# Attention scores: one fp32 product of q and k in place of three f32r products of split values

## The chip, the cores and the metric

The kernel runs on one core of one Trainium2 chip. The metric is the device time of one execution in microseconds; the median of three runs is given.

## The reference

Three layers follow one another: attention with normalised q and k, a gated feed-forward layer, and a soft mixture of experts. Only the first lines matter here:

```python
q_n, k_n = (rmsnorm(q, g_q), rmsnorm(k, g_k))          # q, k: 4 x 12 x 448 x 64
scores = scale * np.matmul(q_n, k_n.transpose(0, 1, 3, 2))
scores = scores - np.max(scores, axis=-1, keepdims=True)
attn = np.exp(scores)
attn = attn / (np.sum(attn, axis=-1, keepdims=True) + 1e-09)
return np.matmul(attn, v).astype(np.float32)
# then x (1792 x 768) -> silu(x @ w_gate) * (x @ w_val) @ w_out  (d_ff 1536) -> soft MoE, 8 experts, 4 slots each
```

## The kernel before

**Attention.** The 4 batches x 12 heads are worked on in 24 pairs of heads (`pairs`, index i). A pair has four steps c = 0..3, one for each block of query rows (three of 128 rows, a last of 64), so there are 96 attention steps t = 4i + c. The two heads of a pair lie in partitions 0 to 63 and 64 to 127 (`halves`). For a block with c < 3 the scores of the two heads are two matmuls that use the two halves of TensorE's rows (L493), each with 64 rows of contraction, 128 weight columns and 448 moving columns. For c = 3 the last 64 query rows of both heads stand in one zero-padded tile `qz`, and one matmul with 128 rows serves both heads (L497).

**The split.** f32r is a matmul type that keeps fewer bits of a 32-bit float. To keep precision, q and k are each stored as a high part, as f32r rounds it, and a low part (the value minus the high part). `qa` and `ka` hold two planes, high and low, and `scores` adds up three products a block: high x high, high x low, low x high. Per pair, after TensorE has transposed q and k into PSUM (`tq`, L424), `transp_hi` writes the high planes with ScalarE (L454 for q with the gain, L456 for k), and `transp_lo` writes the low planes with VectorE (L465 for q, and L65 inside `sub_lo` for k) and then copies the last 64 columns of both planes of q into `qz` (L474; in the first twelve pairs one half by VectorE and one by GpSimd, later both by GpSimd). The PSUM tile `tq` is one of three that rotate (`pt_tile`); the transposes of the probabilities (`tp`, L572) use the same three, so they wait until both parts have read `tq`.

**After the scores.** VectorE takes the negated row maximum (`smax`, L508), ScalarE the exponential (`sexp`, L520). In the first 12 pairs TensorE transposes the probabilities (L572) and the product with v runs at L595; in the later 12 pairs VectorE transposes and the product runs at L630.

**Order of the work.** It is written out by hand: each step is a list of short names (`ORDA`, `ORD0`, `ORDB` for the steps t < 28, `ORD1` and the following lists afterwards), in which S is `scores`, TH is `transp_hi`, TL or L is `transp_lo`, TP or T the transposes of q and k. Each engine works through its instructions in this order. In steps t < 28 the kernel also rebuilds the feed-forward weights from their 64-bit form on ScalarE, GpSimd (`hneg` L213, `hpos` L219) and VectorE (`raw` L228), and stores them. From t = 28 on (`M0`) each step also runs one block of the feed-forward layer: 18 f32r matmuls with 128 x 128 weights and 448 columns (`gv`, L696). After the 96 attention steps the feed-forward steps go on alone, and last come the experts, whose weights stream in from memory.

Of the kernel before, what the change touches and what calls it, by code (L numbers as in the profile page):

```python
# [8 lines left out]
F32 = mybir.dt.float32  # L9
F32R = mybir.dt.float32r  # L10
# [4 lines left out]
AF = mybir.ActivationFunctionType  # L15
ALU = mybir.AluOpType
# [5 lines left out]
def attn_moe_softmoe_kernel(  # L22
# [15 lines left out]
    nc = tc.nc  # L38
    B, H, S, HD = q.shape
# [5 lines left out]
    P = 128  # L45
    CP = 112
    NC = S // CP
    NP = H // 2
# [9 lines left out]
    EV = dict(v=nc.vector.tensor_copy, a=nc.scalar.copy, p=nc.gpsimd.tensor_copy)  # L58
# [5 lines left out]
    def sub_lo(dst, src, hi):  # L64
        nc.vector.tensor_tensor(out=dst, in0=src, in1=hi.bitcast(F32), op=ALU.subtract)  # L65
# [13 lines left out]
    def s_tile(n):  # L79
        return ps.tile([P, S], F32, tag=f"s{n}", name="s")  # L80
# [10 lines left out]
    ap_ = tc.alloc_tile_pool(name="attn", bufs=1, side="right")  # L91
# [6 lines left out]
    gsc = cpool.tile([P, 1], F32, name="gsc")  # L98
# [203 lines left out]
    NPR = len(pairs)  # L302
    NT_ = NPR * NC
    st = {}
# [11 lines left out]
    NX = 2 * NP  # L316
# [113 lines left out]
    halves = [slice(0, HD), slice(HD, P)]  # L430


    QL = S % P
    qz = [ap_.tile([P, 2, 2 * QL], F32R, name=f"qz{n}") for n in range(2)]

    def qz_zeros():
        for n in range(2):
            nc.vector.memset(qz[n].bitcast(F32), 0.0)

    def qk_tiles(i):  # L440
        d = st[i]
        if "qa" not in d:
            d["qa"] = ap_.tile([P, 2, S], F32R, tag="qa", name="qa", bufs=2)
            d["ka"] = ap_.tile([P, 2, S], F32R, tag="ka", name="ka", bufs=2)
        return d["qa"], d["ka"]

    def transp_hi(i, n):

        if i >= NPR:
            return  # L450
        tq = st[i]["qk"[n]]
        qa, ka = qk_tiles(i)
        if n == 0:
            nc.scalar.activation(out=qa[:, 0], in_=tq[:, :S], func=AF.Copy, scale=gsc[:, 0:1])  # L454
        else:
            (EV[ENG["hid"]] if i < NP else nc.scalar.copy)(out=ka[:, 0], in_=tq[:, :S])  # L456

    def transp_lo(i, n):

        if i >= NPR:  # L460
            return
        tq = st[i].pop("qk"[n])
        qa, ka = qk_tiles(i)
        if n == 0:
            nc.vector.scalar_tensor_tensor(  # L465
                out=qa[:, 1],
                in0=tq[:, :S],
                scalar=gsc[:, 0:1],
                in1=qa[:, 0].bitcast(F32),
                op0=ALU.mult,  # L470
                op1=ALU.subtract,
            )
            for j, r in enumerate(halves):
                EV[ENG["qz"][j] if i < NX else "p"](out=qz[i % 2][r, :, QL * j : QL * j + QL], in_=qa[r, :, S - QL :])  # L474
        else:
            sub_lo(ka[:, 1], tq[:, :S], ka[:, 0])

    def scores(t):

        i, c = divmod(t, NC)  # L480
        d = st[i]
        qa, ka = qk_tiles(i)
        if t < M0 and t % 2:
            sc = [ps.tile([P, S], F32, tag=g, name="s") for g in "gv"[: both(t)]]
        elif t < M0 or i >= NX:
            sc = [s_tile(j) for j in range(2)]
        else:
            sc = [s_tile((2 * (t - M0) + j) % 3) for j in range(2)]
        terms = ((0, 0), (0, 1), (1, 0))
        for n, (wt, mv) in enumerate(terms):  # L490
            if c < NC - 1:
                for j, r in enumerate(halves):
                    nc.tensor.matmul(  # L493
                        sc[j], qa[r, wt, c * P : (c + 1) * P], ka[r, mv, :], start=(n == 0), stop=(n == 2)
                    )
            else:
                nc.tensor.matmul(sc[0], qz[i % 2][:, wt], ka[:, mv], start=(n == 0), stop=(n == 2))  # L497
        d[c] = {"sc": sc, "sm": ap_.tile([P, 2], F32, tag="sm", name="sm", bufs=4), "pr": {}}

    def both(t):  # L500

        return 1 if t % NC == NC - 1 else 2
# [631 lines left out]
    def step0(t):  # L1134
# [8 lines left out]
        def S_():  # L1143
            if t + 1 < M0:
                scores(t + 1)
# [30 lines left out]
        def TH():  # L1176
            if 0 <= ct_ < 2:
                transp_hi(i + 1, ct_)

        def TL():  # L1180
            if 0 <= ct_ < 2:
                transp_lo(i + 1, ct_)
# [101 lines left out]
    def step(t):  # L1284
# [48 lines left out]
        def S_():  # L1333
            if att:
                scores(t)
# [5 lines left out]
        def TH():  # L1341
            if ev is not None:
                transp_hi(i + 1, ev)

        def L_():
            if ev is not None:
                transp_lo(i + 1, ev)
# [208 lines left out]
    ENG = dict(rel0="ap", rel1="aa", top0="p", top1="pp", wl1="pv", wh1="a", hid="a", pvd="avavavaa", pvd1="vavavava", nm="pp", qz="vp", rb="a", xh="a", wpa="aa", wpq="a")  # L1556
# [32 lines left out]
    with tc.manual_schedule():  # L1589
        load(0, "qk")  # L1590
        load(1, "qk")
        setup()
        setup_stack()
        qz_zeros()
        fill(16)
        loads = dict(
# [14 lines left out]
        for n in range(2):  # L1611
            norm_mul(0, n, nc.vector)
            transp(0, n)
            transp_hi(0, n)
            fill(PF[n])
            if n == 0:
                norm_ss(1, (1,))
        load(2, "qk")
        w_load(2)
        for n in range(2):  # L1620
            norm_rs(1, (n,))
            norm_mul(1, n, nc.gpsimd)
            transp_lo(0, n)
        w_relu(0, (0,))
        scores(0)
        fill(4)
        for t in range(NT_ + 4):
            step(t)
            if t == 4:
                for n in range(4):  # L1630
                    nc.sync.dma_start(
                        out=ph32[32 * n : 32 * n + 32], in_=phi.rearrange("(d a) s -> a d s", a=32)
# [30 lines left out]
    with tc.manual_schedule():  # L1663
# [18 lines left out]
        for c in range(KD):  # L1682
# [4 lines left out]
                start=True,  # L1687
                stop=True,
# [68 lines left out]
        for u, (e, i, n) in enumerate(eunits):  # L1757
            w = wtile.pop(u)
            if i == 0:
                if n == 0:  # L1760
                    hacc[e] = s_tile(e % 3)[:, :FQ]
                for c in range(KD2 * n, KD2 * n + KD2):
                    for j in range(4):
                        if e < E - 2:

                            mv = w(c % KD2, 2 * FQ * (j // 2), 2 * FQ)
                            mv = mv.rearrange("p (q a t) -> p a q t", a=2, t=2)[:, j % 2]
                        else:
                            mv = w(c % KD2, FQ * j, FQ)
# [3 lines left out]
                if n == 1:  # L1773
# [10 lines left out]
                    for t in range(2):  # L1784
                        nc.vector.tensor_copy(
                            out=h1m.rearrange("p (j t) s -> p t j s", t=2)[:, t, :, SPE * e : SPE * e + SPE],
                            in_=ht_[:, P * t : P * t + P].rearrange("p (j s) -> p j s", j=4)[
                                :, :, SPE * e : SPE * e + SPE
                            ],
                        )  # L1790
                    h1s[e] = h1m
            else:
                if i == 1:
                    for kh_ in range(KH2 * n, KH2 * n + KH2):
                        for j in range(4):
# [4 lines left out]
                                start=(e == 0 and kh_ == 0),  # L1800
                                stop=(e == E - 3 and kh_ == KH - 1),
# [56 lines left out]
```

## Time and profile before

| | us |
|---|---|
| median of 3 runs | 763.62 (762.92 to 764.35) |
| profiled execution, its own time | 762.68 |
| span of the profiled execution, first to last instruction | 760.8 |
| TensorE busy in the span | 726.9 (96%) |
| VectorE busy | 463.4 (61%) |
| ScalarE busy | 392.2 (52%) |
| GpSimd busy | 439.4 (58%) |
| mean granted TensorE clock | 0.993 of full speed |

Busy time of TensorE counts each matmul from its start to the modelled end of its result, so consecutive matmuls overlap in the record. The time that a matmul costs in a dense stream is therefore read from start to start, not from its duration.

### The profile page before, as it was taken

To read this page: it belongs to the slowest core of one execution; us is meant where nothing else is said; L and a number is where in the kernel's file an instruction comes from. 1 tells how busy PE (TensorE), PEld (TensorE's weight loads), DVE (VectorE), ACT (ScalarE), POOL (GpSimd) and SP (SyncE) were. 2 spreads that over 40 slices of the span, in tenths; PEclk is the share of its full clock that TensorE was granted. 3 is DMA by queue.
4 is the path that set the end of the run, shared out by engine and by line. 5 is a ranking of instruction groups with operands and counts; after the bars stand their busy time and mean duration, and the time that the engine had idled before them with its cause. 6 is when DMAs were issued, how large, how long until landed. Compare 5 with 4: busy or idle time off the path is not lost.

```text
span 760.8 us, 20681 instructions
## 1 busy us (share of the span) xinstructions
PE 726.9 (96%) x8580; PEld 566.5 (74%) x8580; DVE 463.4 (61%) x914; ACT 392.2 (52%) x839; POOL 439.4 (58%) x382
## 2 busy tenths in 40 slices
PE   7899999999999999999999999999999999888884
PEld 6566667787778777888888788888879888655552
DVE  5989988788877866677677777666234123420013
ACT  5888888887788644455444454544232222300112
POOL 8978867766676965778686775844444443000100
PEclk9999999999999999999999999999999999999998
DMA  7677576746675642544335432444247997899998
GB/s 234 193 238 227 181 226 212 224 158 202 212 252 172 195 124 70 156 146 126 92 113 157 145 83 74 124 133 133 85 142 254 384 384 245 314 425 421 413 368 262
DMA packets 74237, 157.84 MB, mean 207 GB/s; under 512 B 9376, under 2 KB 49312, under 8 KB 71328
## 3 DMA queue, kind: packets, MB, share of 16 engines
q1 hardware_dynamic: 73424, 155.49, 61.2%
q8 instruction: 67, 1.10, 0.6%
q10 hardware_dynamic: 720, 1.03, 0.4%
q14 instruction: 26, 0.21, 0.1%
HBM read 136.84 MB, written 19.66 MB: 206 GB/s over the span
## 4 chain that ended last, share of the span: by engine, by line
PE 77%; DMA 9%; POOL 5%; DVE 4%; issue 3%; ACT 1%; ACTq 0%; SPq 0%; POOLq 0%; DVEq 0%
PE pg L696 44%; DMA w<-in_moe_w_dram 7%; PE s L493 6%; PE xp L630 6%; PE tp L572 3%; PE tq L424 2%; PE s L595 2%; PE sp L887 2%; POOL hpos L219 2%; PE xp L595 2%; PE s L497 1%; POOL ri L392 1%; PE lp L770 1%; PE wpp L268 1%; PE s L1770 1%
## 5 line engine op out<-in xcount | busy, mean ns | idle before, releaser
L696 PE MATMUL pg<-xh,wh 128*128 128x448 f32 x576 | 219.3, 381 | 0.0
L696 PE MATMUL pg<-xl,wh 128*128 128x448 f32 x576 | 210.8, 366 | 0.0
L520 ACT ACTIVATE pr<-s,sm 128x448 f32<-128x448 f32 x168 | 106.2, 635 | 113.3 <-DVE sm L508 109.5
L696 PE MATMUL pg<-xh,wl 128*128 128x448 f32 x432 | 158.5, 367 | 0.3 <-POOL wl L255 0.3
L696 PEld LDWEIGHTS pg<-xh,wh 128*128 128x128 f32 x576 | 108.2, 188 | 21.9 <-issue 10.0
L255 POOL TENSOR_TENSOR wl<-raw,wh 128x768 fp32r<-128x768 f32 x60 | 111.1, 1861 | 11.1 <-ACT wh L247 10.9
L696 PEld LDWEIGHTS pg<-xl,wh 128*128 128x128 f32 x576 | 108.5, 188 | 8.6 <-issue 0.6
L247 ACT CAST wh<-raw 128x768 fp32r<-128x768 f32 x96 | 79.0, 836 | 58.9 <-PE pg L696 34.9
L537 POOL TENSOR_SCALAR pr<-pr,su 128x448 f32<-128x448 f32 x84 | 54.8, 663 | 81.5 <-DVE su L533 35.1
L508 DVE TENSOR_REDUCE sm<-s 128x1 f32<-128x448 f32 x168 | 98.0, 613 | 2.3 <-PE s L493 1.0
L219 POOL TENSOR_TENSOR hpos<-hpos,hneg 128x768 f32<-128x768 f32 x36 | 66.1, 1835 | 40.1 <-ACT hneg L210 35.7
L696 PEld LDWEIGHTS pg<-xh,wl 128*128 128x128 f32 x432 | 81.1, 188 | 7.5 <-POOL wl L255 0.7
L255 POOL TENSOR_TENSOR raw<-raw,wh 128x768 fp32r<-128x768 f32 x23 | 42.4, 1843 | 54.0 <-ACT wh L247 54.0
L392 POOL TENSOR_TENSOR ri<-ss,mhalf 128x16 f32<-128x16 f32 (+2 forms) x26 | 70.5, 2712 | 2.2
L493 PE MATMUL s<-ka,qa 64*128 64x448 f32 x432 | 63.3, 397 | 0.4 <-DVE ka L65 0.2
L725 DVE SCALAR_TENSOR_TENSOR ht<-ht,pg 128x448 f32<-128x448 f32 x40 | 24.7, 619 | 60.2 <-ACT ht L718 60.2
L616 DVE STREAM_TRANSPOSE pT<-pr 128x448 f32<-128x448 f32 x84 | 52.8, 628 | 5.1 <-POOL pr L537 4.8
L572 PE MATMUL tp<-ident,pr 128*112 128x128 f32 x336 | 49.8, 278 | 5.6 <-DVE qa L465 2.0
L696 PE MATMUL pg<-xh,raw 128*128 128x448 f32 x144 | 52.7, 366 | 0.0
L572 PEld LDWEIGHTS tp<-ident,pr 128*112 128x112 f32 x336 | 36.1, 133 | 21.9 <-issue 7.2
L493 PEld LDWEIGHTS s<-ka,qa 64*128 64x128 f32 x432 | 34.9, 184 | 21.1 <-issue 11.7
L398 POOL TENSOR_TENSOR qn<-qk,ri 128x512 f32<-128x512 f32 (+1 forms) x46 | 50.1, 1090 | 0.9
(216 smaller groups left out, 1162.4 us busy)
## 6 DMA issues: line engine op xcount, KB each, us to landing
w<-in_moe_w_dram SPq DMA_DIRECT2D x22, 1536.0 KB, 12.6
raw<-w SPq DMA_DIRECT2D x72, 384.0 KB, 5.4
w<-raw SPq DMA_DIRECT2D x36, 384.0 KB, 3.2
vt<-in_v_dram SPq DMA_DIRECT2D x60, 224.0 KB, 4.0
r<-in_moe_w_out_dram SPq DMA_DIRECT2D x12, 768.0 KB, 5.0
r<-in_moe_w_gate_dram SPq DMA_DIRECT2D x12, 768.0 KB, 6.2
r<-in_moe_w_val_dram SPq DMA_DIRECT2D x12, 768.0 KB, 5.1
w<-in_moe_w_dram SPq DMA_DIRECT2D x24, 384.0 KB, 9.8
```

The costliest lines, as they stand in the source:

```text
L219: eng.tensor_tensor(out=hp, in0=hp, in1=hn, op=ALU.subtract)
L247: (EV[ENG["wh1"]] if u - NO < NU else nc.scalar.copy)(out=wh, in_=wst[u]["raw"])
L255: eng.tensor_tensor(out=wl, in0=wst[u]["raw"], in1=wst[u]["wh"].bitcast(F32), op=ALU.subtract)
L392: nc.gpsimd.tensor_tensor(out=ri, in0=ss, in1=mhalf[:p, : len(ns)], op=ALU.pow)
L398: eng.tensor_tensor(out=st[i]["qn"][:, n].rearrange("p c h d -> p h c d"), in0=st[i]["qk"][: rows(i), n], in1=st[i]["ri"][:, n] .rearrange ...
L493: nc.tensor.matmul(sc[j], qa[r, wt, c * P : (c + 1) * P], ka[r, mv, :], start=(n == 0), stop=(n == 2))
L508: nc.vector.tensor_reduce(out=d["sm"][:, j : j + 1], in_=d["sc"][j], axis=AX.X, op=ALU.max, negate=True)
L520: nc.scalar.activation(out=p, in_=d["sc"][j], func=AF.Exp, bias=d["sm"][:, j : j + 1], accum_out=st[i]["su"][:, c, j : j + 1])
L537: nc.gpsimd.tensor_scalar(out=p, in0=p, scalar1=su[:, j : j + 1], scalar2=1.0, op0=ALU.mult, op1=ALU.mult)
L572: nc.tensor.transpose(tp[:CP, ck * P : (ck + 1) * P], pr[:, ck * CP : (ck + 1) * CP], ident)
L616: nc.vector.transpose(out=pT[:, 6 - c if j else c, :], in_=st[i][c]["pr"].pop(j))
L696: nc.tensor.matmul(d[r], wt[:, P * c : P * c + P], mv, start=(c == 0 and n == 0), stop=(c == KD - 1 and n == 2),)
```

## The change

q and k are written once each, by ScalarE, as plain fp32 (`transp_hi` keeps its two instructions, with fp32 as the output type). The two VectorE instructions that make low parts go. `transp_lo` only copies the last 64 columns of q into `qz`, one plane in place of two, and reads `qa` instead of following the low part; it does nothing for k. `scores` issues one fp32 matmul a head (c < 3) or a block (c = 3), where three f32r matmuls were added up in PSUM. The order lists are as they were. The tiles `qa`, `ka` and `qz` have half their size.

```diff
-    qz = [ap_.tile([P, 2, 2 * QL], F32R, name=f"qz{n}") for n in range(2)]
+    qz = [ap_.tile([P, 2 * QL], F32, name=f"qz{n}") for n in range(2)]
...
-            d["qa"] = ap_.tile([P, 2, S], F32R, tag="qa", name="qa", bufs=2)
-            d["ka"] = ap_.tile([P, 2, S], F32R, tag="ka", name="ka", bufs=2)
+            d["qa"] = ap_.tile([P, S], F32, tag="qa", name="qa", bufs=2)
+            d["ka"] = ap_.tile([P, S], F32, tag="ka", name="ka", bufs=2)
...
     def transp_hi(i, n):
...
         if n == 0:
-            nc.scalar.activation(out=qa[:, 0], in_=tq[:, :S], func=AF.Copy, scale=gsc[:, 0:1])
+            nc.scalar.activation(out=qa, in_=tq[:, :S], func=AF.Copy, scale=gsc[:, 0:1])
         else:
-            (EV[ENG["hid"]] if i < NP else nc.scalar.copy)(out=ka[:, 0], in_=tq[:, :S])
+            (EV[ENG["hid"]] if i < NP else nc.scalar.copy)(out=ka, in_=tq[:, :S])
 
     def transp_lo(i, n):
...
-            nc.vector.scalar_tensor_tensor(
-                out=qa[:, 1],
-                in0=tq[:, :S],
-                scalar=gsc[:, 0:1],
-                in1=qa[:, 0].bitcast(F32),
-                op0=ALU.mult,
-                op1=ALU.subtract,
-            )
-            for j, r in enumerate(halves):
-                EV[ENG["qz"][j] if i < NX else "p"](out=qz[i % 2][r, :, QL * j : QL * j + QL], in_=qa[r, :, S - QL :])
-        else:
-            sub_lo(ka[:, 1], tq[:, :S], ka[:, 0])
+        if i >= NPR or n:
+            return
+        qa, ka = qk_tiles(i)
+        for j, r in enumerate(halves):
+            EV[ENG["qz"][j] if i < NX else "p"](out=qz[i % 2][r, QL * j : QL * j + QL], in_=qa[r, S - QL :])
...
-        terms = ((0, 0), (0, 1), (1, 0))
-        for n, (wt, mv) in enumerate(terms):
-            if c < NC - 1:
-                for j, r in enumerate(halves):
-                    nc.tensor.matmul(
-                        sc[j], qa[r, wt, c * P : (c + 1) * P], ka[r, mv, :], start=(n == 0), stop=(n == 2)
-                    )
-            else:
-                nc.tensor.matmul(sc[0], qz[i % 2][:, wt], ka[:, mv], start=(n == 0), stop=(n == 2))
+        if c < NC - 1:
+            for j, r in enumerate(halves):
+                nc.tensor.matmul(sc[j], qa[r, c * P : (c + 1) * P], ka[r, :], start=True, stop=True)
+        else:
+            nc.tensor.matmul(sc[0], qz[i % 2], ka, start=True, stop=True)
```

## Rows read from the trace of the kernel before

**Rows 1.** The page's part 1: busy us (share of span), instructions of two engines.
```profile
PE 726.9 (96%) x8580; PEld 566.5 (74%) x8580; DVE 463.4 (61%) x914; ACT 392.2 (52%) x839; POOL 439.4 (58%) x382
```

**Rows 2.** Stretches: length; PE, PEld, DVE, ACT, POOL busy us (count); clock; DMA share; GB/s.
```profile
11.00:32.00 21.00, 16.25 (x141) 11.20 (x139) 17.90 (x28) 17.95 (x40) 19.72 (x18) 1.00 0.62 198
32.00:43.00 11.00, 9.81 (x76) 6.23 (x76) 9.63 (x18) 9.16 (x21) 8.78 (x9) 1.00 1.00 278
43.00:113.00 70.00, 68.96 (x1023) 45.77 (x1021) 64.56 (x110) 60.38 (x145) 55.09 (x42) 1.00 0.69 214
113.00:530.00 417.00, 416.64 (x4791) 336.44 (x4790) 304.74 (x608) 248.55 (x531) 290.95 (x253) 1.00 0.49 151
...
655.00:760.80 105.80, 83.32 (x1522) 52.30 (x1514) 18.59 (x57) 16.64 (x41) 4.76 (x12) 0.95 0.97 370
```

**Rows 3.** Groups by line, TensorE: output<-inputs, rows*columns, output xcount | busy us, mean ns | idle.
```profile
L493 PE MATMUL s<-ka,qa 64*128 64x448 f32 x432 | 63.3, 397 | 0.4 <-DVE ka L65 0.2 <-ACT ka L456 0.2
...
L497 PE MATMUL s<-ka,qz 128*128 128x448 f32 x72 | 19.7, 382 | 0.0
```

**Rows 4.** Timeline of TensorE around one block of scores (c < 3): start us, us, what.
```profile
259.61 0.37 PE L696 MATMUL pg<-xh,wl 128*128 128x448 f32 x1
259.90 0.88 PE L493 MATMUL s<-ka,qa 64*128 64x448 f32 x6
260.71 0.47 PE L696 MATMUL pg<-xh,wh 128*128 128x448 f32 x1
261.02 0.37 PE L696 MATMUL pg<-xl,wh 128*128 128x448 f32 x1
```

**Rows 5.** Timeline of TensorE around one block of scores with c = 3.
```profile
264.51 0.76 PE L497 MATMUL s<-ka,qz 128*128 128x448 f32 x3
265.11 0.36 PE L696 MATMUL pg<-xh,wh 128*128 128x448 f32 x1
```

**Rows 6.** Timeline of TensorE around the two first fp32 matmuls of L794.
```profile
278.89 1.02 PE L794 MATMUL lt<-lg,stack 128*128 128x448 f32 x2
...
279.95 0.37 PE L696 MATMUL pg<-xl,wh 128*128 128x448 f32 x1
...
559.21 0.36 PE L696 MATMUL pg<-xh,raw 128*128 128x448 f32 x1
559.41 0.91 PE L794 MATMUL lt<-lg,stack 128*128 128x448 f32 x2
...
560.36 0.36 PE L696 MATMUL pg<-xl,wh 128*128 128x448 f32 x1
```

**Rows 7.** Timeline of TensorE: fp32 matmuls of L1740 in four tiles of 32 rows.
```profile
747.79 0.42 PE L1740 MATMUL op<-ext,w 32*112 32x192 f32 x2 [0.32 <-DVE w L1747]
747.80 0.41 PE L1740 MATMUL s<-ext,w 32*112 32x192 f32 x1
747.81 0.56 PE L1740 MATMUL op<-ext,w 32*112 32x192 f32 x3
748.06 0.32 PE L1740 MATMUL s<-ext,w 32*112 32x192 f32 x1
```

**Rows 8.** Timeline of TensorE, 10 to 116 us: entries with idle time before them [us <-releaser].
```profile
32.08 1.08 PE L572 MATMUL tp<-ident,pr 128*112 128x128 f32 x8 [1.23 <-ACT pr L520]
42.54 0.62 PE L572 MATMUL tp<-ident,pr 128*112 128x128 f32 x4 [1.11 <-DVE qa L465]
65.06 0.62 PE L572 MATMUL tp<-ident,pr 128*112 128x128 f32 x4 [0.36 <-DVE hT L583]
```

**Rows 9.** Groups by line, VectorE, 10 to 110 us: the two that make low parts.
```profile
L465 DVE SCALAR_TENSOR_TENSOR qa<-tq,gsc,qa 128x448 fp32r<-128x448 f32 x8 | 5.4, 680 | 1.7 <-ACT qa L454 1.7
L65 DVE TENSOR_TENSOR ka<-tq,ka 128x448 fp32r<-128x448 f32 x8 | 4.9, 610 | 0.5 <-ACT ka L456 0.5
```

**Rows 10.** Timeline of VectorE at 41 us: an instruction and the wait before it.
```profile
40.84 0.96 DVE L228 SCALAR_TENSOR_TENSOR raw<-r,hpos 128x768 uint32<-128x768 uint32 x1 [1.21 <-POOL hpos L219]
```

**Rows 11.** Groups by line, GpSimd, 10 to 110 us: the copies into `qz`.
```profile
L474 POOL CAST qz<-qa 64x128 fp32r<-64x128 f32 x8 | 2.3, 288 | 10.0 <-DVE qa L465 9.8
```

More of the change, by code (lines that the diff above doesn't have):

```diff
@@ L433, in attn_moe_softmoe_kernel @@
     QL = S % P
-    qz = [ap_.tile([P, 2, 2 * QL], F32R, name=f"qz{n}") for n in range(2)]
+    qz = [ap_.tile([P, 2 * QL], F32, name=f"qz{n}") for n in range(2)]
     def qz_zeros():
         for n in range(2):
-            nc.vector.memset(qz[n].bitcast(F32), 0.0)
+            nc.vector.memset(qz[n], 0.0)
     def qk_tiles(i):
@@ L442, in qk_tiles @@
         if "qa" not in d:
-            d["qa"] = ap_.tile([P, 2, S], F32R, tag="qa", name="qa", bufs=2)
-            d["ka"] = ap_.tile([P, 2, S], F32R, tag="ka", name="ka", bufs=2)
+            d["qa"] = ap_.tile([P, S], F32, tag="qa", name="qa", bufs=2)
+            d["ka"] = ap_.tile([P, S], F32, tag="ka", name="ka", bufs=2)
         return d["qa"], d["ka"]
     def transp_hi(i, n):
[L449 to L453, printed above, removed]
-            nc.scalar.activation(out=qa[:, 0], in_=tq[:, :S], func=AF.Copy, scale=gsc[:, 0:1])
-        else:
-            (EV[ENG["hid"]] if i < NP else nc.scalar.copy)(out=ka[:, 0], in_=tq[:, :S])
-    def transp_lo(i, n):
         if i >= NPR:
@@ L464, in transp_lo @@
         if n == 0:
-            nc.vector.scalar_tensor_tensor(
-                out=qa[:, 1],
-                in0=tq[:, :S],
-                scalar=gsc[:, 0:1],
-                in1=qa[:, 0].bitcast(F32),
-                op0=ALU.mult,
-                op1=ALU.subtract,
-            )
-            for j, r in enumerate(halves):
-                EV[ENG["qz"][j] if i < NX else "p"](out=qz[i % 2][r, :, QL * j : QL * j + QL], in_=qa[r, :, S - QL :])
-        else:
-            sub_lo(ka[:, 1], tq[:, :S], ka[:, 0])
+            nc.scalar.activation(out=qa, in_=tq[:, :S], func=AF.Copy, scale=gsc[:, 0:1])
+        else:
+            (EV[ENG["hid"]] if i < NP else nc.scalar.copy)(out=ka, in_=tq[:, :S])
+    def transp_lo(i, n):
+        if i >= NPR or n:
[3 more added lines that the diff above has]
+            EV[ENG["qz"][j] if i < NX else "p"](out=qz[i % 2][r, QL * j : QL * j + QL], in_=qa[r, S - QL :])
     def scores(t):
```

## The prediction

> **What bounds the kernel now.** I read the page's busy times first: TensorE 96%, VectorE 61% [rows 1]. Such a mean hides stages, so the second view is the busy time by stretch [rows 2]. From 113 to 530 us, where attention and the feed-forward layer run together, TensorE is busy 416.64 of 417.00 us; from 43 to 113 us, the later steps of the head, 68.96 of 70.00. Only before 43 us has it gaps: 4.75 us between 11 and 32 us, 1.19 us between 32 and 43 us. There GpSimd (19.72 of 21.00 us) and VectorE (17.90) are the full ones. After 655 us the kernel waits for expert weights (DMA share 0.97). So work taken from VectorE pays only before 43 us, and time added to TensorE is paid almost everywhere the scores run. Busy is not proof of a dense stream, as ends are modelled, so the third view is the timeline, read from start to start; in it the f32r matmuls of L696 follow each other at about 0.205 us (261.02 to the row after a block, less the load that is named below) [rows 4].
>
> **The price of a block of scores, before.** For c < 3 six matmuls run as three passes, two heads side by side in TensorE's row halves: from the block's first start, 259.90, to the next matmul's, 260.71, is 0.81 us [rows 4]. It splits into 3 passes of about 0.205 (0.615 us) and 0.19 us at the two ends. For c = 3 three matmuls follow the stream with no gap: 264.51 to 265.11, 0.60 us [rows 5]. There are 432 / 6 = 72 blocks of the first kind and 72 / 3 = 24 of the second [rows 3], four a pair of heads.
>
> **The price after.** An fp32 matmul with 448 columns is not in the scores yet, but L794 is one: 128 x 128 weights, 448 columns, two records. In the middle of a stream the f32r matmul before it starts at 559.21, it starts at 559.41, and the second f32r matmul after it starts at 560.36 [rows 6]. From 559.41 to 560.36 is 0.95 us, of which one f32r pass takes 0.205: the fp32 matmul costs 0.745 to 0.75 us, 0.375 a record. That is the c = 3 block as it will be: 0.75 - 0.605 = +0.145 us.
>
> For c < 3 the question is whether the two heads still run side by side and whether the 0.1 us at each end stays. Side by side: the four row tiles of L1740 are fp32, and records of four different tiles start between 747.79 and 747.81 us, the next at 748.06 [rows 7]; so row tiles overlap in fp32. The ends: the other L794 matmul comes straight after a row-tiled block, and takes 278.89 to 279.95 with one f32r pass, 1.06 us, 0.105 more than in the stream [rows 6]; that is the load of the first weights that nothing covers once the tiling changes, and fp32 does not hide it. So both ends stay, and the block goes from 0.615 to 0.75 us of passes: +0.14 us. The number of weight loads falls from three to two a tile, but they lie under the passes in both kernels (next paragraph).
>
> The Trainium skill (TensorE: Matmul & The Clock Gate, section Part 3: Packing small matmuls, The mechanism) says that a weight load overlaps matmuls in flight only when it goes to another row group. By that rule every pass would pay its load, and two long passes with two loads would cost what three short passes with three loads cost. The trace does not agree: the f32r matmuls of one tile start 0.205 us apart with a load each, and L794's two records take 0.75 us together [rows 4, 6].
>
> **How many blocks pay.** From 32.08 us on TensorE has hardly a gap, so a block behind that point moves everything behind it. Steps 7 to 95 lie there: 66 blocks with c < 3 and 23 with c = 3. 66 x 0.143 + 23 x 0.145 = 12.8 us (0.143 is the middle of 0.135, from 0.75 less 0.615, and 0.15, from 0.75 less 0.60). The six blocks of steps 1 to 6 fall where TensorE waits for others and cost nothing; if that cover were gone they would cost 6 x 0.143 = 0.9 us.
>
> **What comes back.** VectorE loses 24 x 2 instructions, 0.68 and 0.61 us each [rows 9], 31 us in all, and the copies into `qz` are halved. In the stretch from 113 to 530 us VectorE is busy 304.74 of 417.00 us and TensorE waits for nobody [rows 2], so 17 of the 24 pairs give nothing back. In the head I take the waits one by one [rows 8]:
> - 42.54 us, 1.11 us, the transposes of probabilities wait until the low part of q has read the PSUM tile. The low part goes, the tile is free once ScalarE has read it, and TensorE itself is the next late one: -1.1 us.
> - 65.06 us, 0.36 us, and one more wait of the same kind 28 us later: they wait for a VectorE copy in a run of VectorE work that holds low parts: 2 x 0.36, -0.7 us.
> - 32.08 us, 1.23 us, and the smaller waits before it (4.75 us of gaps between 11 and 32 us [rows 2]): they end on ScalarE or GpSimd, and GpSimd is busy 19.72 of 21.00 us. VectorE's own rebuild of weights waits for GpSimd too, 1.21 us at 40.84 us [rows 10]. GpSimd loses at most half of each copy into `qz`, 0.14 of 0.288 us [rows 11], and three of them lie before 40 us: at most 0.4 us. Its waits for the low part of q in front of these copies, 9.8 us in all [rows 11], end sooner, but GpSimd's gaps in the stretch to 32 us are only 1.3 us [rows 2]. If all gaps to 32 us went instead, 4.75 us less the 0.9 us of passes would come back, 3.8 us; if nothing, 0. I take -0.3, near zero, since GpSimd keeps its work.
>
> ScalarE keeps its two instructions a pair at the same shapes; a plain fp32 output instead of a rounded one I cost at nothing between -0.05 and +0.05 us each, and ScalarE (248.55 of 417.00 us, [rows 2]) hides it. `scores` no longer waits for VectorE but for ScalarE, which is earlier in every step; no wait is added and no queue is passed. The stage after 530 us has no score work; its weight stream starts when attention's memory comes free, so it moves along with TensorE.
>
> Sum: 12.8 - 1.1 - 0.7 - 0.3 = +10.7 us. The profiled execution took 762.68 us (span 760.8 and 1.9 around it), so 773.4 after; the median of the runs lies 0.94 us above the profiled one, so I predict 763.62 + 10.7 = 774.3 us. The forecast's own range: all gaps of TensorE from 11 us on recovered (4.75 + 1.19 + 1.04 = 7.0 us against 95 blocks, 13.6 us) gives +6.6, 770.2; nothing recovered and nothing covered gives +13.7, 777.3.
>
> **The rivals.**
> - *The load at the block's border is hidden under a longer fp32 pass* in 64-row tiles. Then 0.105 us of each c < 3 block comes back: 12.8 - 66 x 0.105 - 2.1 = +3.8 us, 767.4. For: a record of 0.375 us is longer than a load. Against: L794 after a row-tiled block still pays 0.105 us [rows 6].
> - *The head is bound by VectorE* and shrinks by what VectorE loses, so the kernel is not slower. From 10 to 110 us the low parts are 5.4 + 4.9 us [rows 9], and half of eight copies into `qz` is an estimated 8 x 0.14 = 1.1 us at GpSimd's price [rows 11], 11.4 us; only the 68 blocks of steps 28 to 95 would pay, 9.8 us: -1.6 us, 762.0. For: VectorE is busy 64.56 of 70.00 us from 43 to 113 us [rows 2]. Against: TensorE is busy 68.96 us of the same 70.00, and shows 7.0 us of gaps in the whole head. It decides from the point where the head gives back more than 1.4 us a pair (9.8 / 7).
> - *Loads are not covered in fp32 row tiles or in f32r ones*, the rule named above as a mechanism of this kernel: three passes of 0.187 and three loads of 0.187 us (0.375 / 2 as the clean pass) make 1.12 us, two records and two loads the same, so the passes cost nothing and only the 2.1 us come back: 761.5. The rows speak against it.
> - *The two heads no longer overlap in fp32.* Then each c < 3 block takes 0.75 us more: 10.7 + 66 x 0.75 = +60 us, 834. L1740 speaks against it [rows 7].
> - *The product is not carried out as two fp32 records* but in a single pass: 89 x 0.41 us less than before, about 727. L794 and L1740 speak against it [rows 6, 7].
>
> **How the numbers follow.** The forecast gets 0.83, the border rival 0.07, VectorE's head 0.03 (at the edge: half of it faster by over 0.2%, half within), the load rule 0.02 (faster), the loss of overlap 0.03, the single pass 0.01, and 0.01 is left. A change of 0.2%, 1.5 us, is about what a measurement of this kernel can tell from none. So faster 0.05, same 0.02, slower 0.93. The range reaches from 767.0, which takes in the border rival, to 778.0, just past the forecast's upper end.
>
> **What would show it.** In the profile after, the scores should have 288 records of 64 rows and 48 of 128 rows in place of 432 and 72; a c < 3 block among L696 should take 0.95 us from its first start to the next matmul in place of 0.81, a c = 3 block 0.75 in place of 0.60. The stretch of steps 28 to 95 should be 9.8 us longer, VectorE's busy time some 31 us shorter, and step 10's scores should start close to where they did, 43.5 us. TensorE should still have no gap after that. If the stretch from step 28 to 95 grows by less than 6 us, the price of the passes is wrong; if it grows as said and the total does not, the head gave back more than its gaps.

## The result and the profile after

The changed kernel takes 771.12 us in the median of six runs, the kernel before 763.27 us in the runs beside it: a ratio of 1.0097, with an interval from 1.0071 to 1.0123. A second series of both gave 1.0123 (1.0102 to 1.0144). So the change costs 7 to 9 us, about 1%. The profiled execution after took 773.55 us, the longest of its six, with a span of 771.8 us.

The page's part 1 after the change shows TensorE 11.3 us busier and VectorE 26.3 us less busy than [rows 1]:

```profile
PE 738.2 (96%) x8412; PEld 547.7 (71%) x8412; DVE 437.1 (57%) x866; ACT 391.3 (51%) x839; POOL 441.4 (57%) x382
```

Busy times by stretch after, in the columns of [rows 2]; 114.8 us is now the start of step 28 and 540 us that of step 95, where they were 113 and 530:

```profile
11.00:32.00 21.00, 16.82 (x128) 10.02 (x126) 16.78 (x23) 17.32 (x37) 19.73 (x18) 1.00 0.64 190
32.00:43.00 11.00, 10.17 (x73) 6.00 (x74) 9.31 (x17) 8.86 (x23) 10.44 (x9) 1.00 1.01 300
43.00:114.80 71.80, 70.95 (x990) 42.22 (x987) 58.84 (x102) 60.45 (x145) 57.90 (x42) 1.00 0.68 207
114.80:540.00 425.20, 425.01 (x4668) 323.24 (x4668) 286.33 (x574) 248.14 (x531) 288.36 (x253) 1.00 0.49 148
666.00:771.80 105.80, 82.82 (x1544) 51.95 (x1515) 18.96 (x58) 17.02 (x42) 4.77 (x12) 0.97 0.98 373
```

Before 32 us GpSimd is as full as it was, 19.73 us against 19.72. From 43 us on TensorE has no more room than before; the stretch with the feed-forward steps has grown by 8 us with TensorE full in both. The last row is cut to the length of the one before; its busy times are alike, and from step 95 to the end it takes 232.1 us where it took 231.6.

VectorE was forecast to lose some 31 us. The 48 instructions that went had records of 30.7 us together, as costed; records of successive instructions overlap, so busy time falls by less, and its copies into `qz` took 6.7 us where they took 3.1.

The two groups of score matmuls after (columns as in [rows 3]): two fp32 records a product, 72 x 2 x 2 = 288 and 24 x 2 = 48.

```profile
L479 PE MATMUL s<-ka,qa 64*128 64x448 f32 x288 | 73.6, 588 | 0.2 <-ACT ka L456 0.2
...
L481 PE MATMUL s<-ka,qz 128*128 128x448 f32 x48 | 22.2, 544 | 0.0
```

Timeline of TensorE after, around one block with c < 3 and one with c = 3 (as [rows 4] and [rows 5]):

```profile
264.22 1.02 PE L479 MATMUL s<-ka,qa 64*128 64x448 f32 x4
265.18 0.47 PE L680 MATMUL pg<-xh,wh 128*128 128x448 f32 x1
...
268.96 0.91 PE L481 MATMUL s<-ka,qz 128*128 128x448 f32 x2
269.37 0.71 PE L680 MATMUL pg<-xh,wh 128*128 128x448 f32 x1
269.92 0.36 PE L680 MATMUL pg<-xl,wh 128*128 128x448 f32 x1
```

The first block takes 264.22 to 265.18, 0.96 us where it was 0.81 (over the 51 such blocks of steps 28 to 95, medians of 0.953 and 0.806): the two heads still run side by side, and the uncovered time at the ends is still there. For the second, 268.96 to 269.92 less one f32r pass of 0.205 is 0.755 us where it was 0.60.

The waits of TensorE in the head after (as [rows 8]; those above 0.6 us between 20 and 120 us, complete):

```profile
24.93 0.60 PE L424 MATMUL tq<-ident,qn 112*128 112x112 f32 x4 [1.65 <-POOL qn L398]
...
32.83 1.09 PE L556 MATMUL tp<-ident,pr 128*112 128x128 f32 x8 [2.14 <-ACT pr L504]
45.92 0.65 PE L556 MATMUL tp<-ident,pr 128*112 128x128 f32 x4 [0.67 <-ACT pT L567]
```

The waits at 42.54, 65.06 and 93.48 us are gone; behind 45.92 us the timeline shows none up to step 28. The one at 32 us is longer (1.23 us before), the one that ends on GpSimd near 24 us has grown from 0.32 to 1.65 us, and a new one ends on ScalarE at 45.92 us.

Where the time lies: the first score matmuls of steps 28 and 95, before and then after.

```profile
113.05 0.47 PE L493 MATMUL s<-ka,qa 64*128 64x448 f32 x2
...
529.15 0.36 PE L497 MATMUL s<-ka,qz 128*128 128x448 f32 x1
```

```profile
114.81 0.65 PE L479 MATMUL s<-ka,qa 64*128 64x448 f32 x2
...
539.67 0.54 PE L481 MATMUL s<-ka,qz 128*128 128x448 f32 x1
```

The same two starts from every profile, us:

| kernel | start of step 28 | start of step 95 | steps 28 to 95 | step 95 to the end | span |
|---|---|---|---|---|---|
| before | 113.05 | 529.15 | 416.1 | 231.6 | 760.8 |
| before, again | 114.64 | 530.42 | 415.8 | 230.4 | 760.8 |
| after | 114.81 | 539.67 | 424.9 | 232.1 | 771.8 |
| after, again | 117.69 | 541.79 | 424.1 | 230.5 | 772.2 |
| low parts kept | 115.60 | 540.07 | 424.5 | 229.7 | 769.8 |
| qz copy on ScalarE | 114.17 | 538.93 | 424.8 | 230.2 | 769.2 |
| phi loads later | 114.29 | 538.39 | 424.1 | 232.0 | 770.4 |
| low parts gone, three f32r products | 119.20 | 534.27 | 415.1 | 230.8 | 765.1 |
| four f32r products | 116.20 | 544.99 | 428.8 | 229.6 | 774.6 |
| one f32r product | 108.70 | 508.68 | 400.0 | 230.4 | 739.0 |
| fp16 split | 112.71 | 523.40 | 410.7 | 229.8 | 753.2 |
| fp16 split, phi loads later | 114.72 | 524.42 | 409.7 | 231.1 | 755.5 |

The middle column is steady to 1 us among kernels with the same score products. Nearly all of that 1 us lies in steps 42 and 43, which take 11.3 to 12.1 us in the profiles with the fp32 product. The columns beside it scatter by 1 to 4 us from one execution to the next. In the last column the profile after is the longest of the fp32 kernels; at the start of step 28 it is in their middle, and the first profile before is the earlier of its two.

### The profile page after: what moved, and what is told of

Its sections match the earlier page's. It is cut to its first block, busy times and chain, and to the rows that moved or that the text cites. A ratio compares the mean times of both kernels' runs of the same rounds, so it can differ in the third digit from the quotient of the medians.

```text
span 771.8 us, 20295 instructions
## 1 busy us (share of the span) xinstructions
PE 738.2 (96%) x8412; PEld 547.7 (71%) x8412; DVE 437.1 (57%) x866; ACT 391.3 (51%) x839; POOL 441.4 (57%) x382
## 4 chain that ended last, share of the span: by engine, by line
PE 82%; DMA 9%; POOL 3%; issue 2%; ACT 1%; SPq 1%; DVE 1%; ACTq 0%; POOLq 0%; DVEq 0%
PE pg L680 45%; PE s L479 8%; DMA w<-in_moe_w_dram 7%; PE xp L614 6%; PE tp L556 4%; PE tq L424 2%; PE s L579 2%; PE s L481 2%; PE xp L579 2%; PE sp L871 2%; PE lp L754 1%; PE wpp L268 1%; PE rb L539 1%; PE s L1754 1%; DMA r<-in_moe_w_out_dram 1%
## 5 line engine op out<-in xcount | busy, mean ns | idle before, releaser
L680 PE MATMUL pg<-xh,wh 128*128 128x448 f32 x576 | 223.6, 388 | 0.0
L255 POOL TENSOR_TENSOR wl<-raw,wh 128x768 fp32r<-128x768 f32 x60 | 112.5, 1886 | 11.1 <-ACT wh L247 11.0
L479 PE MATMUL s<-ka,qa 64*128 64x448 f32 x288 | 73.6, 588 | 0.2 <-ACT ka L456 0.2
L255 POOL TENSOR_TENSOR raw<-raw,wh 128x768 fp32r<-128x768 f32 x23 | 42.4, 1843 | 54.2 <-ACT wh L247 51.5
L614 PEld LDWEIGHTS xp<-pT,vt 32*64 32x64 f32 x2688 | 39.6, 130 | 11.4 <-issue 10.9
```

The source lines that it names most:

```text
L255: eng.tensor_tensor(out=wl, in0=wst[u]["raw"], in1=wst[u]["wh"].bitcast(F32), op=ALU.subtract)
L479: nc.tensor.matmul(sc[j], qa[r, c * P : (c + 1) * P], ka[r, :], start=True, stop=True)
L614: nc.tensor.matmul(xp[g][HD * h : HD * h + HD, :P], vt[r, h, j, :], pT[r, slice(6, 2, -1) if h else slice(0, 4), QB * jj : QB * jj + QB], ...
L680: nc.tensor.matmul(d[r], wt[:, P * c : P * c + P], mv, start=(c == 0 and n == 0), stop=(c == KD - 1 and n == 2),)
```

## The experiments

**The two kernels once more.** No edit.

> The changed kernel as it is, once more. The first profile after showed a span 11.0 us longer than before, the median of the times only 7.9 us. Theory A (the passes cost 12.8 us less 2 us of recovered waits, and runs scatter by 2 to 3 us in the head): the second profile again shows step 95 of the scores 10 to 11 us later than in the kernel before, or, if this execution is a quick one, the difference lies before step 28 and the stretch from step 28 to 95 is again 9 to 10 us longer. Theory B (the passes cost only 7 to 8 us): the stretch from step 28 to 95 is 6 us longer in this profile.

> The kernel before, once more, to see how its own trace scatters. Theory A: from step 28 on the same distances between starts within 0.2 us in all; before step 28 the two profiles may differ by 1 to 2 us. Theory B: the whole trace repeats within 0.3 us.

Measured: 771.50 us after and 762.42 us before. Steps 28 to 95 take 8.0 to 9.1 us more after than before, over the four pairs of profiles. That lies between the two theories' numbers and nearer to the first. From the start of step 28 to that of step 95 lie 67 blocks, not 68, or 9.6 us at the prediction's prices: 0.5 to 1.6 us too much in the sum. Before step 28 the second profile after is 2.9 us later than the first. Its timeline shows a wait of TensorE, and the stretch with that wait a lower clock:

```profile
47.40 1.10 PE L556 MATMUL tp<-ident,pr 128*112 128x128 f32 x4 [2.00 <-ACT pT L567]
```

```profile
41.00:44.50 3.50, 3.50 (x26) 1.78 (x22) 3.50 (x7) 1.12 (x4) 3.23 (x3) 1.00 1.08 354
44.50:50.00 5.50, 3.50 (x19) 1.44 (x25) 2.38 (x7) 4.85 (x12) 5.17 (x5) 0.75 0.69 245
```

TensorE stood idle for 2.00 us of the 5.5, and the granted clock of that stretch is 0.75 of full speed: part of it, from 47.3 to 50.7 us, ran at 0.50 of full speed, 1.2 GHz. The kernel before also did not repeat as either theory said: its second profile is 1.6 us later at step 28 and 1.3 us quicker behind step 95, with the same span.

**Low parts kept.** The fp32 product, but VectorE's two instructions stay; their output is read by nothing.

```diff
-        if i >= NPR or n:
+        if i >= NPR:
             return
+        tq = st[i].pop("qk"[n])
         qa, ka = qk_tiles(i)
+        lo = ap_.tile([P, S], F32R, tag=f"lo{n}", name=f"lo{n}", bufs=2)
+        if n:
+            sub_lo(lo, tq[:, :S], ka)
+            return
+        nc.vector.scalar_tensor_tensor(
+            out=lo, in0=tq[:, :S], scalar=gsc[:, 0:1], in1=qa, op0=ALU.mult, op1=ALU.subtract
+        )
...
```

> One fp32 product a block as in the change, but VectorE still makes both low parts (into tiles that nothing reads), so the passes are paid and nothing comes back from VectorE. Theory A (the head gives back little): 1 to 2 us above the changed kernel, 771.5 to 773.5. Rival (VectorE bounds the head, and its relief is worth some 11 us): about 782.

Measured: 772.44 us, a ratio of 1.0133 (1.0112 to 1.0154), 0.9 us above the changed kernel's second series and 1.3 above its first. The intervals of the two ratios overlap (1.0123 has 1.0102 to 1.0144), so VectorE's relief is worth between nothing and some 3 us, and not 11. The waits on VectorE are back in TensorE's timeline:

```profile
42.36 0.62 PE L564 MATMUL tp<-ident,pr 128*112 128x128 f32 x4 [0.77 <-DVE lo L468]
...
66.16 0.62 PE L564 MATMUL tp<-ident,pr 128*112 128x128 f32 x4 [0.49 <-DVE hT L575]
```

**Low parts gone, three f32r products.** The other half alone: the changed kernel with f32r tiles and three products, all of the high parts. The low parts are left out of the scores, which come out three times as large.

```diff
+    NTERM = 3
...
-            d["qa"] = ap_.tile([P, S], F32, tag="qa", name="qa", bufs=2)
-            d["ka"] = ap_.tile([P, S], F32, tag="ka", name="ka", bufs=2)
+            d["qa"] = ap_.tile([P, S], F32R, tag="qa", name="qa", bufs=2)
+            d["ka"] = ap_.tile([P, S], F32R, tag="ka", name="ka", bufs=2)
...
+        for n in range(NTERM):
...
+                        sc[j], qa[r, c * P : (c + 1) * P], ka[r, :], start=(n == 0), stop=(n == NTERM - 1)
```

> The other half alone: no low parts are made and three f32r products are added up, all three of the high parts (so the low parts are left out of the scores, and the scores are three times as large). Theory A: VectorE's relief alone is worth the head's waits, 1 to 2 us, so 761 to 762.5. Rival (VectorE bounds the head): about 752. In this kernel the copy of the last columns of q still has the f32r output type.

Measured: a ratio of 1.0005 (0.9968 to 1.0041), from times of 758.67 to 769.72 us. The rival's 752 us is out. That the relief gains 1 to 2 us is not shown by this run, as its times scatter too widely; the quickest is 1.5 us below the quickest of before in the same series, 760.20 us. For the products this kernel is the nearest control, as VectorE makes no low parts in it either: the changed kernel's steps 28 to 95 are 9.0 to 9.8 us longer than its 415.1, where the prices give 9.6. The profile shows one way in which the gain is lost. From a wait of 2.14 us on, TensorE's clock is low (0.67 of full speed in the last stretch, which holds full TensorE work):

```profile
110.25 1.52 PE L268 MATMUL wpp<-wlh,hT 32*32 32x128 f32 x58 [2.14 <-issue]
```

```profile
105.00:113.00 8.00, 5.86 (x162) 3.91 (x145) 5.47 (x10) 5.33 (x14) 5.37 (x4) 0.86 0.56 169
113.00:120.00 7.00, 7.00 (x48) 5.17 (x44) 2.41 (x4) 3.02 (x6) 0.00 (x0) 0.67 0.25 86
```

**One and four f32r products.** The same kernel with `NTERM` at 1 or 4 in place of 3.

> A single f32r product of the high parts, no low parts (so two of the three products are left out of the scores). Theory A (TensorE bounds steps 28 to 95, a pass costs 0.205 us): that stretch is 68 x 0.41 = 28 us shorter than in the kernel before, about 388 us, and the whole 30 to 36 us shorter, 727 to 732. Rival (another engine is close behind TensorE there): the stretch shrinks by less than 20 us and TensorE shows gaps.

> Four f32r products of the high parts a block, no low parts (so the scores are four times as large and the low parts are left out). It has four passes, as the fp32 product is said to have, at the f32r pass of 0.205 us. Theory A (the pass's time counts, not the kind of product): steps 28 to 95 take 68 x 0.205 = 14 us more than with three products, some 429 us, and the whole is about 8 us slower than the changed kernel, 778 to 781. Rival (fp32 costs what four passes cost): equal to the changed kernel, 771.

Four products: 777.46 us, 1.0197 (1.0176 to 1.0218), and steps 28 to 95 take 428.8 - 415.1 = 13.7 us more than with three, as the first theory said (14); the whole is 0.5 us below the range that it gave. The blocks:

```profile
266.95 1.08 PE L481 MATMUL s<-ka,qa 64*128 64x448 f32 x8
267.96 0.47 PE L684 MATMUL pg<-xh,wh 128*128 128x448 f32 x1
...
271.76 0.96 PE L485 MATMUL s<-ka,qz 128*128 128x448 f32 x4
272.56 0.36 PE L684 MATMUL pg<-xh,wh 128*128 128x448 f32 x1
```

1.01 and 0.80 us: each pass adds 0.20 us to the block, and the block's time goes on to the whole. An fp32 product (0.96 and 0.755 us) lies between three and four f32r passes. One product: 744.93 us, two runs only, 0.9764 (0.9711 to 0.9817). Steps 28 to 95 shrink by 416.1 - 400.0 = 16 us, not the 28 of the first theory; the rival's numbers were right here. TensorE shows gaps, 7.06 us in the stretch, where before it had 0.36:

```profile
108.70:508.70 400.00, 392.94 (x4550) 315.78 (x4550) 289.51 (x574) 247.22 (x530) 288.12 (x251) 1.00 0.52 157
```

So TensorE is the bound on the side of more work, and the room below it is smaller than its blocks suggest. That another engine is close behind is not shown: only 1.8 us of these gaps end on ScalarE or GpSimd, the rest (5.3 us) stand in front of the product with v and end on TensorE's own scores or on nothing that the profile shows.

**fp16 split.** The kernel before, with high and low parts in fp16.

```diff
-    qz = [ap_.tile([P, 2, 2 * QL], F32R, name=f"qz{n}") for n in range(2)]
+    qz = [ap_.tile([P, 2, 2 * QL], F16, name=f"qz{n}") for n in range(2)]
...
-            d["qa"] = ap_.tile([P, 2, S], F32R, tag="qa", name="qa", bufs=2)
-            d["ka"] = ap_.tile([P, 2, S], F32R, tag="ka", name="ka", bufs=2)
+            d["qa"] = ap_.tile([P, 2, S], F16, tag="qa", name="qa", bufs=2)
+            d["ka"] = ap_.tile([P, 2, S], F16, tag="ka", name="ka", bufs=2)
...
```

> The kernel before with high and low parts in fp16 in place of f32r, three products as before. The f32r passes start 0.205 us apart where 448 columns need 0.187 us (half an fp32 record). Theory A (an f32r pass waits for its own weight load, 0.184 to 0.188 us and some 0.018; the weight load of a 16-bit tile is 0.109 us in the trace, so it hides): a pass takes 0.187 us and the uncovered first load of a c < 3 block shrinks from 0.105 to some 0.03 us, 66 x 0.13 + 23 x 0.054 = 9.8 us less, about 753. Rival (0.205 us is the price of 448 columns in any type): 762.

Measured: 755.82 us, 0.9906 (0.9892 to 0.9921), quicker than both kernels, and 3 us above the 753 that the first theory gave. The block with c < 3:

```profile
257.24 0.74 PE L494 MATMUL s<-ka,qa 64*128 64x448 f16 x6
257.92 0.47 PE L697 MATMUL pg<-xh,wh 128*128 128x448 f32 x1
```

0.68 us in place of 0.81, the 0.13 us that the first theory gave. The weight loads of this line (count: min/median/max ns) are 94 ns, half of an f32r load of 184:

```profile
L494 PEld LDWEIGHTS <-qa x432: 92/94/112, 11.5 to 519.2; 64*128 64x128 f16 x144
```

Steps 28 to 95 shrink by 5.1 to 5.4 us, and by 6.1 to 6.4 in the profile with the phi loads later; the blocks' 0.13 and 0.054 us would make 7.5. As with one product, not all that TensorE gives up reaches the whole.

**qz copy on ScalarE.** The changed kernel, the first half of the copy by ScalarE.

```diff
-    ENG = dict(..., qz="vp", ...)
+    ENG = dict(..., qz="ap", ...)
```

> The changed kernel with the first half of the qz copy in the first twelve pairs on ScalarE in place of VectorE. In the profiles after, VectorE's plain fp32 copy into qz took 2.73 and 1.17 us at step 4 (0.19 us elsewhere) because a GpSimd instruction ran. Theory A (the wait is hidden, as VectorE's next instruction waits for the same GpSimd work): no change that can be measured, 770 to 772. Rival (this wait ate the gain of the head): 1 to 2 us faster than the changed kernel, and the start of step 10 about 1 us earlier.

Measured: 770.51 us, 1.0102 (1.0087 to 1.0117). The start of step 10 is 42.35 us where it was 43.22 and 43.48 in the two profiles after, as the rival said (though the four-product kernel, whose copy stays on VectorE, starts it at 42.34), but the whole does not differ by more than the intervals: the wait of the copy did not eat the head's gain to an extent that this shows.

**phi loads later.** The changed kernel, and the fp16 split, with the four loads of phi two steps later.

```diff
-            if t == 4:
+            if t == 6:
```

> The changed kernel with the four loads of phi issued after step 6 in place of step 4. In all profiles of the changed kernel ScalarE waits 2.3 to 5.2 us in the head for a transfer of the out weights, which it did not in the first profile of the kernel before; these transfers stand in SyncE's queue behind the four phi loads, whose issue takes 4 us. Theory A (this transfer is what is late next in the head once VectorE is relieved): ScalarE's wait for it shrinks below 1 us, step 10 starts 0.5 to 1 us earlier, and the whole is 1 to 2 us faster than the changed kernel, 769 to 770. Rival (the transfer is late for another reason, or GpSimd holds the head anyway): 770.5 to 771.5, as the changed kernel.

> The fp16 split (three products of high and low parts, as in the kernel before, in fp16) with the phi loads after step 6. Theory A: low parts are made here, so VectorE and not the transfer is late in the head; equal to the fp16 split alone within 1 us, 755 to 756.5. Rival: 1 to 2 us faster, 754.

What led to it: ScalarE's waits between 10 and 114 us in the first and the second profile after (us in total, times, longest).

```profile
ACT hpos L210 <- DMA r<-in_moe_w_out_dram: 2.3, 1, 2.3
```

```profile
ACT hpos L210 <- DMA r<-in_moe_w_out_dram: 5.2, 2, 3.0
```

Measured: the wait shrinks to 1.3 us, but the time is 772.52 us, 1.0145 (1.0108 to 1.0183), no quicker: the first theory failed. With the fp16 split: 759.02 us, 0.9975 (0.9942 to 1.0008) where it was 0.9906 without the move, with runs from 755.49 to 766.76; both theories failed, and what made it slower is open. The late transfer is a wait that took the place of VectorE's in the head, but it is not shown that it costs time.

## Why the prediction was right, point by point

- *The bound.* TensorE from 43 us on, GpSimd before 32 us. The stretches show it after as before, and a fourth f32r product adds what a pass costs, 0.20 us a block.
- *The price of the passes.* +0.14 to +0.15 us a block, from an fp32 matmul elsewhere in the kernel: 0.96 and 0.755 us measured, +0.15 each. That the ends of the block stay uncovered, that the heads still overlap and that there are two records a product held too, which takes out the rivals of the hidden load, of the lost overlap and of the single pass.
- *How many blocks pay.* Here the sum is a little too large. For steps 28 to 95 it had 9.8 us, or 9.6 from start to start, and 8.0 to 9.1 were measured, though each block costs its price. "TensorE waits for nobody" was not quite so: in step 43 an f32r matmul of the feed-forward layer waits 0.34 us for GpSimd's `wl` (L255) in both profiles before, and 0.19 us and not at all in the two after. There the longer passes ran under a wait that was there anyway. Without steps 42 and 43, the same two starts lie 412.74 to 412.79 us apart in all five profiles with the fp32 product, 403.79 and 404.04 before, and 403.58 with the low parts gone: 8.7 to 9.2 us for 65 blocks, priced at 9.3. What shortened the others is open. The wait in step 43, before and then after:

```profile
215.09 0.47 PE L696 MATMUL pg<-xh,wl 128*128 128x448 f32 x1 [0.34 <-POOL wl L255]
```

```profile
218.52 0.47 PE L680 MATMUL pg<-xh,wl 128*128 128x448 f32 x1 [0.19 <-POOL wl L255]
```

- *What comes back.* The sum gave 2.1 us for the whole head; 21 blocks of steps 7 to 27 should cost 3.0, so step 28 should come 0.9 us later. It comes 1.8 us later in the first pair, and 0.2 to 1.8 us later in the pairs whose clock was full in the head. This term was too large: from 11 us to step 28 TensorE's idle time falls by 1.1 us in each pair, from 6.98 to 5.86 us in the first and from 8.18 to 7.13 in the second. With the low parts kept it is 5.95 us, so not even these 1.1 us are shown to be VectorE's. The wait at 42.54 us vanished as said; the next late was not TensorE alone, as the step put it: in the first profile after ScalarE waits 2.28 us for a transfer, until 43.66 us, and TensorE 0.67 us for ScalarE behind it.
- *The rival of VectorE's head* fell: 64.56 of 70 us busy, and yet its relief gains nothing that stands clear of the scatter, and not 11 us.
- *The rival of the uncovered loads* fell with the block times.
- *The total.* 10.7 us forecast, 7 to 9 measured in the medians, 11.0 between the first two profiles. The last agrees by luck: that profile after was the slowest of its runs, and in this pair the blocks of steps 28 to 95 cost 0.9 us less than the sum had, the head gave back 0.9 us less, and from step 95 to the end it took 0.5 us longer.

A step that failed, without harm that a time shows: the copies into `qz` were taken as halved. GpSimd's went from 0.29 to 0.24 us in the median, VectorE's from 0.22 to 0.19 or more, and VectorE's timeline after shows one of them at 2.73 us:

```profile
19.75 0.95 DVE L228 SCALAR_TENSOR_TENSOR raw<-r,hpos 128x768 uint32<-128x768 uint32 x1
...
26.24 2.73 DVE L464 COPY qz<-qa 64x64 f32<-64x64 f32 x1 [0.57 <-ACT qa L454]
```

GpSimd's timeline at the same time:

```profile
19.70 1.06 POOL L391 TENSOR_SCALAR ss<-ss 112x16 f32<-112x16 f32 x1
...
27.11 1.81 POOL L219 TENSOR_TENSOR hpos<-hpos,hneg 128x768 f32<-128x768 f32 x1
```

The copy, 0.19 us at its shortest, ends when GpSimd's `hpos` is done (28.92 us). And GpSimd's `ss`, 0.21 us in the profile before, takes 1.06 when it starts beside VectorE's `raw`, which begins earlier now that VectorE has less to do: GpSimd, the bound of that stretch, loses 0.85 us, and the wait of TensorE behind it at 24.93 us is 1.65 us. In the second profile after, `ss` took 0.21 us. The Trainium skill (SBUF — State Buffer, section Who interferes with whom) says that a VectorE instruction with two inputs in SBUF contends with a GpSimd instruction that reads SBUF, and that one in a mode that uses two ports, which a copy or a cast can enter when its operands allow it, blocks the other or is blocked for the whole instruction. These rows agree. Not every row does: in the profile before, `raw` starts at 21.13 us while GpSimd's `ri` runs (20.08 to 22.98) and takes 0.95 us, as in the row above.

## What to carry to other kernels

Price a product by the start-to-start time of its passes in the bounding engine, read from an instruction of the same type and size that is already in the trace; here an fp32 matmul elsewhere gave the block's price to 0.01 us. Work taken off an engine that is not the bound of its stretch returns little: 31 us of VectorE's work gave back at most some 3 us here, and waits on GpSimd, ScalarE and a transfer stood where VectorE's had been. Where passes of a split product are the cost, look at what sets the pass: a 16-bit split with the same three products took 1% off this kernel.

## What the runs showed of the hardware

- f32r passes of 448 columns start 0.205 us apart beside weight loads of 0.184 to 0.188 us. fp16 passes cost 0.68 us a block in place of 0.81, with loads of 0.094 us. That the load sets the f32r pass fits these numbers, but the load was not varied by itself. An fp32 matmul of 448 columns takes two records 0.375 us apart.
- A VectorE copy of 64 x 64 plain fp32 values took 0.19 us at its shortest, and 2.73 us where GpSimd's `qn` and `hpos` ran beside it. The copy before, with an f32r output and 128 columns, took 0.22 us, and beside GpSimd's `hpos` 0.41 and 0.69 us in the two profiles; it too ended just behind `hpos`, so the wait is not shown to come with the output type.
- The granted clock fell to 1.2 GHz for part of a stretch in the head where TensorE had stood idle for 2.00 us (the second profile after), 2.14 us (low parts gone) and 2.53 us (one product; 0.50 of full speed from 31.2 to 38.0 us). In the first profile after, a wait of 2.14 us that ended at 32.83 us did not bring it down.
